# Attention recurrence of an adaLN block: layernorm moved into the loop, weights loaded ahead, deferred transposes cut into single pieces

## The chip, the cores and the metric

One core of one Trainium2 chip. The time is device time in microseconds (us) of one execution of the whole program, forward and backward. A program on one core has no other core to be compared with, so a run counts as slow only if it is over 1.5% above the fastest of the same kernel; every run used below counts as fast, save the single run of e5, whose state is unknown. The engines are TensorE (PE in the profile), VectorE (DVE), ScalarE (ACT), GpSimd (POOL) and SyncE (SP, which here only issues transfers).

## The reference, cut

```python
def _A_ref(x, mem0, Wq, Wk, Wv, Wo, seg_len):        # S=2048, Dm=512, H=32 heads, Dh=128, M=8, seg_len=32
    mem = mem0
    for s in range(n_seg):                           # 64 segments, one after another
        h = concatenate([mem, xs])                   # 8 memory rows + 32 rows of x
        q, k, v = h @ Wq, h @ Wk, h @ Wv
        p = softmax(where(mask, q k^T * scale, -1e9))
        o = (p v) @ Wo
        mem = o[:, :M, :].copy()                     # the next segment needs this
        outs.append(o[:, M:, :])
    return concatenate(outs)

mod = (silu(c) @ w_mod)...                           # sa, ca, ga, sb, cb, gb
h = layernorm(x) * (1 + ca) + sa
x = x + ga * _A_ref(h, ...)
h = layernorm(x) * (1 + cb) + sb
x = x + gb * _B_ref(h, w_gate, w_up, w_down)         # gated MLP
# the kernel returns x and the gradients of eleven inputs for a given grad_out
```

## The kernel before

Five phases matter by name. Phase 0 makes the modulation vectors from `w_mod`. Phase 1 makes the layernorm of all 2048 rows. Phase 2 is the recurrence of 64 segments. Phase 3 is the gated MLP, and what follows is the backward pass. Each phase opens pools of on-chip memory and closes them at its end, so a later phase's tiles lie over an earlier phase's, and a load into them waits until the earlier readers are done (before the change, the first projection waited 43.1 us for Wq, and POOL 8.2 us for a phase 1 transfer before it issued Wv).

```python
    def phase1(self):                                   # all 16 tiles ahead of the first segment
        ...
        for j in range(NT):
            nc.vector.tensor_scalar(xh[:], xall[:, j, :], mv[:, j, 0:1], rstd[:, j:j + 1], ...)
            nc.gpsimd.tensor_tensor(h1a[:], xh[:], ca1_bc[:], op=ALU.mult)
            nc.vector.tensor_tensor(h1[:], h1a[:], sa_bc[:], op=ALU.add)
            ...                                         # 4 transposes, one ACT copy
            nc.sync.dma_start(self.HX[s], hx[:, :, ...])   # to DRAM, one piece per segment

    def phase2(self):
        with ExitStack() as ctx:
            wp = ctx.enter_context(tc.tile_pool(name="p2w", bufs=1))   # over phase 0's and 1's memory
            nc.sync.dma_start(Wq[:], ...)               # 4 MB each
            nc.scalar.dma_start(Wk[:], ...)
            nc.gpsimd.dma_start(Wv[:], ...)
            nc.sync.dma_start(Wo[:], ...)
            ...
            for s in range(NS):
                ...
                nc.gpsimd.dma_start(self.MEMT[s], hT[:, :, 0:M])
                ...
                proj_bank("q", 0, QT, hT, "act")        # 48 matmuls of 40 columns, then an eviction
                proj_bank("k", 0, KT, hT, "dve")
                ...                                     # q1 k1 scores(0) q2 k2 scores(1)
                proj_bank("v", 0, VT, hT, "act"); den(0); st_exp(2)
                proj_bank("v", 1, VT, hT, "act"); den(1)
                proj_bank("v", 2, VT, hT, "act")
                vst(0); den(2); vst(1)                  # transposes of V, copied by DVE
                filler()                                # f_pst: all 3 thirds of P
                vst(2)
                pv(0); pv(1)                            # P times V, normalised by DVE into Ost
                filler()                                # f_qst: all 3 thirds of Q, copied by DVE
                pv(2)
                ott(0)                                  # transposes of Ost, copied by ACT into OT
                filler()                                # f_kst: all 3 thirds of K, copied by DVE
                ott(1); filler(); ott(2)
                outproj(0); outproj(1); outproj(2)
                nc.scalar.activation(hT_next[:, :, 0:M], at_ps[0][:, :, 0:M], AF.Copy)   # the recurrence
                ...                                     # AOT, VT and OT to DRAM
                fillers = mk_fillers()                  # [f_pst, f_qst, f_kst] of this segment
```

A filler is work of the last segment that nothing in the loop needs, kept for a place where TensorE would otherwise wait: transposes of P, Q and K for the backward pass, with a copy and a 384 KB store of each. VT and OT are stored in the same size, so a segment writes 5 x 384 KB, 1.97 MB. Of the names in the profiles, `proj_ps`, `tps`, `or_ps` and `at_ps` are what TensorE writes: projections, transposes, P times V and the output projection. An eviction is the copy of such a result by ACT or DVE. `Vst` is V transposed, `Ost` the normalised P times V, `OT` its transpose, which the output projection reads, and `hT` holds a segment's input rows.

The softmax here doesn't subtract the row's maximum and nothing guards it: scores larger than these inputs give would overflow.

## Time and profile before

| | before |
|---|---|
| time, median of the first 6 runs | 4554.05 us (4544.21 to 4566.25) |
| time, median of 16 runs beside the changed kernel | 4556.27 us |
| profiled execution | 4561.1 us |
| start, to the memory store of segment 1 | 175.8 us |
| 62 segment periods | 22.44 us each |
| border: last memory store to the first row tile of phase 3 | 49.0 us |
| everything after | 2944.8 us |

The last four rows come from the times at which single instructions start; the prediction shows the two memory stores, and the border ends where ACT writes `a_rows` at 1616.32. The granted TensorE clock was 0.50 from 50 to 150 us, and the first projection's matmuls, from 151.57 us on, issued every 33 ns. The loop alone, in the columns of the prediction's table of stretches:

```profile
175.00:1570.00 1395.00, 1216.81 (x38571) 1163.58 (x38568) 552.98 (x1304) 431.33 (x932) 245.58 (x436) 1.00 0.27 94
```

TensorE's waits between 500 and 1300 us, about 36 segments (what waited, for whom, us in total, times, longest):

```profile
PE tps L343 <- DVE Ost L391: 31.8, 72, 0.7
PE proj_ps L331 <- issue: 28.5, 35, 2.0
PE or_ps L389 <- DVE Vst L383: 25.6, 36, 0.7
PE proj_ps L331 <- ACT hT L445: 10.3, 36, 0.3
```

Lines 1, 3 and 4 are dependencies: each occurs once or twice in every segment and is short. Line 2 has no releaser that the profile shows.

### The profile page before, as it was taken

How to read it: one execution, taken by the hardware profiler on the slowest of the kernel's cores; microseconds unless marked ns; L12 is line 12 of the kernel's file. 1: busy time of each engine (PE TensorE's matmuls, PEld its weight loads, DVE VectorE, ACT ScalarE, POOL GpSimd, SP SyncE). 2: the span in 40 equal slices, each digit the busy share in tenths (PEclk: the TensorE clock that was granted, in tenths of full speed). 3: DMA queues.
4: the chain of work that ended last, by engine and by line, in shares of the span. 5: the costliest groups of instructions: out<-in, count | busy, mean ns of one | idle time of the engine just before them, and what ended most of it. 6: DMA issues, size and time to landing. Idle time of an engine off the chain costs nothing. (4 is left out here: it accounts for less than half of the span.)

```text
span 4561.1 us, 189989 instructions
## 1 busy us (share of the span) xinstructions
PE 3818.3 (84%) x87954; PEld 3203.8 (70%) x87954; DVE 1928.3 (42%) x4034; ACT 1498.9 (33%) x2570; POOL 820.2 (18%) x1210
## 2 busy tenths in 40 slices
PE   2588888888888868797878888888888858999996
PEld 1588888888888734453468888888888855666653
DVE  5234434433333455571123333333334326566554
ACT  0233333333333245351132222222222216565553
POOL 3011111111111111242101111111111122222210
PEclk6799999999999989898969999999999979999998
DMA  4522222222222399666754544544545468878773
GB/s 100 196 93 93 97 94 96 97 97 96 93 93 94 113 211 188 216 212 185 192 167 145 158 159 145 159 159 153 165 146 157 156 137 179 164 159 160 158 160 114
DMA packets 633321, 656.43 MB, mean 144 GB/s; under 512 B 429943, under 2 KB 516487, under 8 KB 630733
## 3 DMA queue, kind: packets, MB, share of 16 engines
q1 hardware_dynamic: 552396, 326.23, 29.9%
q0 software_dynamic: 75952, 304.94, 20.2%
q8 instruction: 687, 11.26, 1.1%
q10 hardware_dynamic: 4176, 13.11, 0.8%
q14 instruction: 110, 0.89, 0.1%
HBM read 346.57 MB, written 297.56 MB: 141 GB/s over the span
## 5 line engine op out<-in xcount | busy, mean ns | idle before, releaser
L1193 PE MATMUL gps<-rows,hrows 128*128 128x384 bf16 (+1 forms) x2640 | 461.7, 321 | 4.1 <-ACT ot L61 2.4
L1193 PEld LDWEIGHTS <-hrows 128*128 128x128 bf16 x2640 | 252.7, 98 | 139.3 <-issue 5.9
L1007 PE MATMUL dh_ps<-dKT,WkT 128*128 128x40 bf16 x8192 | 238.2, 183 | 109.9 <-issue 109.8
L1052 DVE CAST dh1T<-dh_ps 128x128 bf16<-128x128 f32 x64 | 18.7, 292 | 733.9 <-ACT dyT L1041 733.9
L331 PE MATMUL proj_ps<-hT,Wq 128*128 128x40 bf16 x8192 | 241.3, 180 | 84.0 <-DMA Wq<-in_A_Wq_dram 43.1
L1007 PEld LDWEIGHTS <-WkT 128*128 128x128 bf16 x8192 | 229.1, 98 | 115.1 <-issue 115.0
L63 DVE CAST KT<-proj_ps 128x480 bf16<-128x480 f32 (+2 forms) x256 | 119.7, 488 | 449.1 <-PE proj_ps L331 449.1
L63 DVE COPY rows<-tpg 128x384 bf16<-128x384 bf16 (+1 forms) x616 | 195.5, 347 | 262.9 <-PE tpg L1186 166.5
L331 PEld LDWEIGHTS <-Wq 128*128 128x128 bf16 x8192 | 228.4, 96 | 92.6 <-issue 92.6
L1007 PE MATMUL dh_ps<-dQT,WqT 128*128 128x40 bf16 x8192 | 240.6, 185 | 27.4 <-issue 26.5
L331 PE MATMUL proj_ps<-hT,Wk 128*128 128x40 bf16 x8192 | 241.1, 180 | 25.2 <-issue 24.6
L1007 PEld LDWEIGHTS <-WqT 128*128 128x128 bf16 x8192 | 232.0, 100 | 30.7 <-issue 30.5
L1007 PE MATMUL dh_ps<-dVT,WvT 128*128 128x40 bf16 x8192 | 238.5, 179 | 6.4 <-issue 6.0
L331 PEld LDWEIGHTS <-Wk 128*128 128x128 bf16 x8192 | 221.6, 96 | 29.0 <-issue 28.8
L331 PE MATMUL proj_ps<-hT,Wv 128*128 128x40 bf16 x8192 | 237.0, 179 | 4.3 <-issue 3.5
L1179 ACT ACTIVATE xr<-xt 128x3072 bf16<-128x3072 bf16 (+1 forms) x44 | 235.2, 5348 | 10.7 <-DMA x<-in_A_x_dram 5.7
L957 PEld LDWEIGHTS <-WoT 128*128 128x128 bf16 x8192 | 218.1, 96 | 26.0 <-issue 24.8
L957 PE MATMUL proj_ps<-dyT,WoT 128*128 128x40 bf16 x8192 | 219.8, 180 | 19.6 <-ACT dyT L1041 18.0
L1186 PEld LDWEIGHTS <-xr 128*128 128x128 bf16 x2560 | 179.9, 98 | 77.8 <-issue 28.2
L1007 PEld LDWEIGHTS <-WvT 128*128 128x128 bf16 x8192 | 226.9, 96 | 7.6 <-issue 7.1
L1186 PE MATMUL tpg<-ident,xr 128*128 128x128 bf16 x2560 | 217.6, 219 | 17.4 <-DVE rows L63 5.8
L331 PEld LDWEIGHTS <-Wv 128*128 128x128 bf16 x8192 | 225.6, 96 | 7.0 <-issue 5.9
(318 smaller groups left out, 7559.0 us busy)
## 6 DMA issues: line engine op xcount, KB each, us to landing
VT<-VT POOLq DMA_DIRECT2D x64, 384.0 KB, 3.2
OT<-OT POOLq DMA_DIRECT2D x64, 384.0 KB, 3.6
PS<-Pst POOLq DMA_DIRECT2D x64, 384.0 KB, 2.6
QST<-Qst POOLq DMA_DIRECT2D x64, 384.0 KB, 2.7
KST<-Kst POOLq DMA_DIRECT2D x64, 384.0 KB, 5.8
OT_l<-OT SPq DMA_DIRECT2D x64, 384.0 KB, 3.7
VT_l<-VT SPq DMA_DIRECT2D x64, 384.0 KB, 4.6
Pst_l<-PS SPq DMA_DIRECT2D x64, 384.0 KB, 5.1
```

Source lines behind the costliest of these rows:

```text
L63: return nc.vector.tensor_copy(out, in_)
L331: nc.tensor.matmul(ps[:, g_, hl * L:(hl + 1) * L], lhsT=Ws[w][:, c, h * E:(h + 1) * E], rhs=hT[:, c, :], start=(c == 0), stop=(c == DC - 1))
L957: nc.tensor.matmul(ps[:, g_, hl * L:(hl + 1) * L], lhsT=WoT[:, c, h * E:(h + 1) * E], rhs=dyT[:, c, :], start=(c == 0), stop=(c == DC - 1))
L1007: nc.tensor.matmul(dh_ps[0][:, c, :], lhsT=WT[:, h, c * 128:(c + 1) * 128], rhs=X[:, g_ * GW + hl * L:g_ * GW + (hl + 1) * L], start=(n_dh ...
L1052: nc.vector.tensor_copy(dh1T[:], dh_ps[0][:, :, M:L])
L1179: nc.scalar.activation(xr[:, 0:cut, :], xt[:, :, 0:cut].rearrange("p s x -> p x s"), AF.Copy)
L1186: nc.tensor.transpose(ps[0:KR, hl, :], xr[:, c0:c0 + 2, :].rearrange("p a s -> p (a s)"), self.ident[:, :])
L1193: nc.tensor.matmul(ps[:, 0:nh * E], lhsT=hrows[0:KR, tp_, c * 128:(c + 1) * 128], rhs=rows[0:KR, tp_, 0:nh * E], start=(tp_ == 0), stop=(t ...
```

## The change

Its intent is to start the recurrence before the whole layernorm is done, and to keep TensorE from waiting in the tail of a segment. Cut to its core:

```diff
+    def p2_early(self):                       # opened ahead of phase 0's pool: memory of its own
+        self.Wq = wp.tile(...); self.Wk = wp.tile(...)
+        self.ca1_bc = ...; self.sa_bc = ...; self.x_first = ...; self.mem0 = ...
+        self.p2tiles = [...]                  # QT KT VT ET Vst Ost OT Pst Qst Kst
+    def issue_early(self):                    # called right behind w_mod's load
+        nc.sync.dma_start(self.x_first[:], ...)
+        nc.sync.dma_start(self.mem0[:], ...)
+        nc.sync.dma_start(self.Wq[:], ...)
+        nc.sync.dma_start(self.Wk[:], ...)
 ...
-    def phase1(self):                         # all 16 tiles, HX through DRAM
+        def p1_tile(j):                       # one tile: 128 rows, 4 segments
+            nc.vector.bn_stats(...); nc.vector.bn_aggr(...); nc.vector.tensor_scalar_add(...)
+            nc.gpsimd.tensor_tensor(rstd[:], ve[:], mhalf[:], op=ALU.pow)
+            nc.vector.tensor_scalar(xh[:], ...)
+            nc.vector.tensor_tensor(h1a[:], xh[:], ca1_bc[:], op=ALU.mult)
+            nc.vector.tensor_tensor(h1[:], h1a[:], sa_bc[:], op=ALU.add)
+            ...                               # 4 transposes
+            for s4 in range(nseg):            # straight into the four segments' hT
+                nc.scalar.activation(t[:, :, cfg.M:cfg.L], tp[:, 0:DC, ...], AF.Copy)
 ...
-            nc.sync.dma_start(Wq[:], ...); nc.scalar.dma_start(Wk[:], ...)
             nc.gpsimd.dma_start(Wv[:], ...)
-            nc.sync.dma_start(Wo[:], ...)
+            nc.gpsimd.dma_start(Wo[:], ...)
 ...
             for s in range(NS):
+                if s % nseg_t == 2 and s // nseg_t + 1 < NT:
+                    p1_tile(s // nseg_t + 1)
                 ...
                 proj_bank("q", 1, QT, hT, "act")
+                filler()                      # P, first third
                 ...
                 proj_bank("q", 2, QT, hT, "act")
+                filler()                      # P, second third
                 ...
-                proj_bank("v", 0, VT, hT, "act")
+                proj_bank("v", 0, VT, hT, "dve")
+                filler()                      # P, last third, and its store
                 ...
-                proj_bank("v", 1, VT, hT, "act")
+                proj_bank("v", 1, VT, hT, "dve")
                 ...
                 vst(1)
+                vst(2)
                 filler()                      # Q, first third
-                vst(2)
                 pv(0)
+                filler()                      # Q, second third
                 pv(1)
+                pv(2)
                 filler()                      # Q, last third, and its store
-                pv(2)
                 ott(0)
                 filler()                      # K, first third
                 ott(1)
-                filler()
                 ott(2)
                 outproj(0); outproj(1); outproj(2)
                 ...                           # ACT copy of the memory rows
+                filler()                      # K, second third
+                filler()                      # K, last third, and its store
 ...
-                            self.evac("dve", part3(Qst, pi), ps[:, :, :])   # and Kst
+                            f_x(QT, Qst, self.QST, pi, "act")               # one third per filler, and Kst
```

## The prediction

> **What bounds the kernel now.** I read, in this order, the 40 slices (where is TensorE idle?), the table of stretches, the waits of the first 160 us, and one segment of the recurrence (phase 2) instruction by instruction. TensorE leads overall:
>
> ```profile
> PE 3818.3 (84%) x87954; PEld 3203.8 (70%) x87954; DVE 1928.3 (42%) x4034; ACT 1498.9 (33%) x2570; POOL 820.2 (18%) x1210
> PE   2588888888888868797878888888888858999996
> PEclk6799999999999989898969999999999979999998
> ```
>
> The change touches the first 14 slices only (phases 0, 1, 2) and the border to phase 3. By stretch (columns: length, busy time and count of each engine, granted clock, DMA share, GB/s):
>
> ```profile
> 0.00:160.00 160.00, 34.22 (x514) 22.54 (x515) 60.55 (x99) 13.46 (x21) 43.92 (x50) 0.62 0.57 173
> 160.00:1590.00 1430.00, 1248.07 (x39479) 1193.23 (x39477) 566.75 (x1337) 443.10 (x957) 249.39 (x443) 1.00 0.27 95
> 1590.00:1640.00 50.00, 16.63 (x90) 8.29 (x86) 18.06 (x35) 13.08 (x23) 8.06 (x15) 0.66 0.91 217
> ```
>
> So 160 us of start hold only 34 us of TensorE work. Then come 64 serial segments at 1248/1430 = 87% with DVE at 40% and ACT at 31%: TensorE is the bound there, and what can be won is its 13% of gaps. Why the start is empty:
>
> ```profile
> PE tp L229 <- DVE h L225: 67.9, 14, 32.7
> PE proj_ps L331 <- DMA Wq<-in_A_Wq_dram: 43.1, 1, 43.1
> POOL Wv L260 <- DMA hT<-HX: 8.2, 1, 8.2
> SPq L528 <- DMA KST<-Kst: 19.7, 2, 19.2
> ```
>
> Line 1 is phase 1, all 16 layernorm tiles before the first segment (61 to 116 us). Line 2: the four 4 MB weights are only issued at about 118 us, and the first projection starts at 151.57. Line 3 says why so late: the pool that holds the weights reuses memory of phases 0 and 1, and even Wv waits for a transfer that has nothing to do with it. Line 4 is the same effect at the border to phase 3. The tail of one segment:
>
> ```profile
> 835.41 0.38 PE L343 MATMUL tps<-ident,VT 128*128 128x128 bf16 x4
> 836.09 0.25 PE L376 MATMUL dc_ps<-ones,ET 128*128 128x1 bf16 x4 [0.30 <-ACT VT L61]
> 837.76 0.83 PE L343 MATMUL tps<-ident,QT 128*128 128x128 bf16 x12
> 839.23 0.38 PE L389 MATMUL or_ps<-Vst,ET 128*128 128x128 bf16 x4 [0.63 <-DVE Vst L383]
> 839.83 0.40 PE L343 MATMUL tps<-ident,Ost 128*128 128x128 bf16 x4 [0.22 <-DVE Ost L391]
> 842.02 0.40 PE L343 MATMUL tps<-ident,Ost 128*128 128x128 bf16 x4 [0.68 <-DVE Ost L391]
> 842.25 3.38 PE L408 MATMUL at_ps<-OT,Wo 128*128 128x40 bf16 x128
> 845.91 1.35 PE L331 MATMUL proj_ps<-hT,Wq 128*128 128x40 bf16 x48 [0.28 <-ACT hT L445]
> ```
>
> The segment runs from 824.26 to 845.91, 21.65 us. A 128-column transpose issues every 0.056 us and a 40-column matmul every 0.025 us; distances between the end of issue and the next start are the real holes: 0.46 before 836.09, 0.80 before 839.23, 0.38, 0.23 (at 840.96), 0.84 before 842.02 and 0.44 before 845.91, together 3.15 us. Pure issue is therefore 18.50 us. This segment has no "issue" holes; the mean period, from one store of the memory rows per segment,
>
> ```profile
> 175.84 0.72 POOL L358 DMA_DIRECT2D MEMT<-hT  x1 [2.25 <-ACT hT L445]
> 1567.30 0.72 POOL L358 DMA_DIRECT2D MEMT<-hT  x1 [1.68 <-ACT hT L445]
> ```
>
> is 1391.46 / 62 = 22.44 us, so irregular "issue" holes add about 0.8 us.
>
> [...] The trace shows 0.50 from 50 to 150 us and 33 ns per matmul at 151.57. [...] The 16.8 MB took about 44 us, some 380 GB/s, over three queues. [...]
>
> **The change part by part.**
>
> *Start.* Wq and Wk get memory of their own and are issued behind w_mod, at about 2 us. w_mod lands at 11.3; 8.4 MB at 380 to 420 GB/s then take 20 to 22 us: Wk is there at about 33. In parallel phase 0 ends with the last modbc copy at 29.3; ca and sa are copied by ACT instead of going through memory; layernorm of tile 0 can go ahead on DVE but for the affine part (two 0.69 us operations), then four transposes, four small copies: hT is ready near 31 to 32. First projection: about 33 us against 151.57. Wv and Wo wait for phase 0's pool, whose last reader is the modbc store; in the queue behind Wk it lands at about 38. Then 8.4 MB in about 21 us: Wv at about 49, Wo at 60. Segment 0 would reach v at 44 (11 us after its start, as before) and its output projection 9 us later, so it is held by both and ends near 63, against 175.3. **Saved: about 112 us.**
>
> *Phase 1 in the loop.* 15 tiles, each on DVE 0.66 + 0.17 + 0.15 + 0.55 + 0.69 + 0.69 = 2.9 us (rows L213, L214, and phase 3's twins L553, L558, L563, L565), 0.56 us of POOL (L555), four ACT copies of about 0.3 us (estimate from L445's 0.20 for a quarter of the columns) and 0.22 us of TensorE. On TensorE 0.06 us per segment. DVE and ACT have room, if the chain runs early. The order of an engine's queue isn't the source's: before, mem0's load (L308, phase 2) was issued at 1.65 us and the phase 2 memsets from 1.87. I expect the tile's DVE work to be moved up into idle time a segment or more ahead, and its transposes to find h1 ready. The HX store and loads vanish.
>
> *Segment.* Removed from DVE: six copies (2 x 1.07 us). Added to it: two V casts (2 x 0.66). Added to ACT: six copies of 0.60, removed two of 0.57. DVE is then near 8.7 us, ACT near 9.4 of some 20 us: neither binds on average. The real change is order. Pst (3 x 0.62) leaves the place ahead of Vst; Qst and Kst leave the place ahead of Ost. I walked the tail with the trace's delays (end of issue to result 0.16, hand-over 0.05 to 0.09). From the last V projection at 0: vst(2) waits for its ACT eviction to 0.75 (hole 0.21); Vst is done at 1.6, pv(2) needs it at 1.85, no hole; Ost results at 2.30, 2.90, 3.50 give holes 0.06, 0.16, 0.38 between the fillers; ACT does Q0, Q1, Q2, OT0, K0, OT1, OT2 one after another from 1.44, so OT0 is out at 3.84, a hole of 0.12 before the output projection at 3.89; OT1 (5.04) and OT2 (5.64) come before they are needed. Together 0.93 instead of 2.71. The two fillers after the output projection (0.44 us) fill the wait for hT almost exactly: 0.02. Period: 18.50 + 0.06 + 0.93 + 0.02 + "issue" 0.9 (a guess: as now, a little more under denser issue) = 20.4. **Saved: 2.04 x 64 = about 130 us.**
>
> *Border to phase 3.* TensorE rests from 1590.3 to 1615.6, since phase 3's tiles lie over Kst and wait for its store, which shares the DMA with 5.4 MB of weights. In the new layout w_gate's and w_up's place is over Wq and Wk, free since the last k projection some 15 us earlier, so the weights can be in flight sooner and the store lands sooner. I book 10 us of the 25.
>
> Sum: 112 + 130 + 10 = 252; 4554 - 252 = **4302 us**.
>
> **The rivals.** (a) *Layernorm on the path*: if the tile's chain stays at its place in the source, it starts behind the last segment's DVE work; about 4.3 us of chain then stand before q of every fourth segment: 15 x 4.5 = 67 us given back, 4370. For: single buffers, and POOL's queue, in which pow could sit behind a store that waits 11.6 us for V. Against: the reordering seen above. One in six. (b) *Fetch-bound*: [...] if "issue" holes grow to 2 us, half the segment gain goes: 4360. For: they sit 3 to 8 us into a segment, when the OT and KST stores run, which stay there. Against: 0.8 us now at nearly full issue. (c) *ACT the new bound in the tail*: seven evictions of 0.60 in a row have 0.6 us of slack at OT2; with one more late, 0.3 to 0.6 us per segment, 4320 to 4340. (d) *Better*: moved-up fillers close the remaining 0.9 us and the border gives 20 us: 4250.
>
> **Range and chances.** The start is worth 105 to 117 and nearly certain. The segment is worth 0.8 to 2.6 us times 64, 50 to 165. The border 0 to 20. That makes 4255 to 4375 for 8 in 10. The 2% line is 4463: even the start alone brings 2.5%, so faster has 0.96.
>
> **What would show it.** First projection between 31 and 36 us and segment 1 starting at 60 to 66: start right. Period from the MEMT stores 20.0 to 20.9, no Vst wait before the last pv, ET/QT/KT transposes in fours: segment right. A TensorE wait of microseconds for h1 in segments 2, 6, 10 would show rival (a); "issue" sums well above 0.8 us per segment rival (b); outproj waiting for ACT OT rival (c). The prediction fails if a wait on memory reuse holds Wq or the first tile as before, or if the period stays above 21.5.

## The result, and the profile after

The changed kernel took 4342.07 us in the median of 8 runs (4333.62 to 4351.64; a ninth, 4362.86, out of the median). The ratio is 0.9527, with a 95% interval from 0.9509 to 0.9546: faster. Here and below a ratio is the mean time of one kernel's fast runs over that of the other's fast runs of the same rounds on the same chip, so it is not quite the ratio of the medians quoted.

Between the two profiled executions, 4561.1 and 4339.9 us, the 221.2 us divide so:

| part | before | after | gained | predicted |
|---|---|---|---|---|
| start, to segment 1 | 175.8 | 69.1 | 106.8 | 112 |
| 62 periods | 22.44 each | 21.00 each | 89.6 | 126 (130 for 64) |
| border | 49.0 | 39.8 | 9.2 | 10 |
| unchanged code after it | 2944.8 | 2929.2 | 15.6 | 0 |

The last row is no gain. The same code took 2912 to 2952 us in the runs below, with no order in it. Between these two profiles the difference is about that of one group, the backward pass's own 40-column matmuls (`dh_ps<-dKT,WkT`): idle time in front of it that the profile calls "issue" was 109.9 us before and 93.7 after.

**The start.** TensorE from 24 to 72 us after the change (start, duration, what, in brackets the idle time before it and what ended it):

```profile
31.23 1.35 PE L347 MATMUL proj_ps<-hT,Wq 128*128 128x40 bf16 x48 [0.36 <-DVE hT L331]
...
32.85 1.37 PE L347 MATMUL proj_ps<-hT,Wk 128*128 128x40 bf16 x48 [0.27 <-DMA Wk<-in_A_Wk_dram]
...
52.34 1.78 PE L347 MATMUL proj_ps<-hT,Wv 128*128 128x40 bf16 x48 [11.84 <-DMA Wv<-in_A_Wv_dram]
...
64.08 4.45 PE L425 MATMUL at_ps<-OT,Wo 128*128 128x40 bf16 x128 [3.12 <-DMA Wo<-in_A_Wo_dram]
```

The first projection starts at 31 us instead of 152. Wk just about arrives in time; Wv costs 11.84 us and Wo 3.12, the two waits that the prediction had put there.

**The loop.** The same instruction as in the prediction's pair of memory stores, and the table's row of the loop:

```profile
69.05 0.73 POOL L375 DMA_DIRECT2D MEMT<-hT  x1 [6.02 <-ACT hT L465]
...
1370.95 0.72 POOL L375 DMA_DIRECT2D MEMT<-hT  x1 [1.74 <-ACT hT L465]
```

```profile
69.00:1370.00 1301.00, 1209.49 (x38482) 1164.85 (x38478) 560.82 (x1137) 551.66 (x1235) 251.74 (x447) 0.98 0.32 102
```

62 periods take 1301.90 us, 21.00 each. TensorE is busy for 93% of them instead of 87%, ACT for 42% instead of 31%, and the granted clock fell from 1.00 to 0.98. One tail, where the prediction shows that of before:

```profile
831.77 0.39 PE L406 MATMUL or_ps<-Vst,ET 128*128 128x128 bf16 x4
831.99 0.39 PE L359 MATMUL tps<-ident,QT 128*128 128x128 bf16 x4
832.22 0.61 PE L406 MATMUL or_ps<-Vst,ET 128*128 128x128 bf16 x8
832.66 0.39 PE L359 MATMUL tps<-ident,QT 128*128 128x128 bf16 x4
...
834.14 0.40 PE L359 MATMUL tps<-ident,Ost 128*128 128x128 bf16 x4 [0.20 <-DVE Ost L408]
834.37 3.38 PE L425 MATMUL at_ps<-OT,Wo 128*128 128x40 bf16 x128
837.60 0.61 PE L359 MATMUL tps<-ident,KT 128*128 128x128 bf16 x8
...
838.26 1.36 PE L347 MATMUL proj_ps<-hT,Wq 128*128 128x40 bf16 x48
```

No line waits for Vst or for the memory rows (hT) any more. One wait for Ost is left, and the output projection follows at once: OT is there. The last eight K transposes stand where TensorE used to wait for hT. By the same arithmetic as in the prediction (distance of starts less 0.0556 us for each 128-column matmul), the holes of this tail from pv on are 0.06, 0.14 and 0.38 us; the walk had 0.06, 0.16 and 0.38, and another 0.12 before the output projection, which is not there. TensorE's waits, same window as before:

```profile
PE proj_ps L347 <- issue: 38.3, 39, 2.7
PE tps L359 <- DVE Ost L408: 7.6, 38, 0.2
PE st_ps L387 <- issue: 3.7, 2, 2.0
```

The dependencies have shrunk to one regular line of 7.6 us. "issue" has grown from 28.5 to 38.3 us on the projections and is now nearly all that is left.

To have one measure for all runs I took, from every pair of neighbouring TensorE matmuls in the loop, the distance of starts less the pure issue time (the distance in an unbroken run at full clock, in these traces 0.025 us for 40 columns, 0.052 for 120, 0.0556 for 128) and summed what exceeds 0.06 us, by releaser. In us per segment:

| | period | waits for DVE | for ACT | "issue" | stretches at half clock in the loop |
|---|---|---|---|---|---|
| before | 22.44 | 2.14 | 0.69 | 1.10 | 2 |
| after | 21.00 | 0.66 | 0.12 | 1.40 | 12 |
| after, a second profile (e12) | 20.68 | 0.68 | 0.12 | 1.13 | 8 |

**The border.** SP issues `w_gate` at 1380.57 us, in the v stage of the last segment, where before it was issued at 1588.29, after the last segment; ACT writes the first `a_rows` at 1410.75 instead of 1616.32.

**What an "issue" hole is.** The longest kind, after the change:

```profile
905.44 0.18 PE L347 MATMUL proj_ps<-hT,Wk 128*128 128x40 bf16 x1
907.80 1.40 PE L347 MATMUL proj_ps<-hT,Wk 128*128 128x40 bf16 x47 [2.17 <-issue]
```

A projection stops after one of its 48 matmuls, in a tile that has all its inputs. Three things in the trace name the place. First, TensorE's 87,954 matmuls with a weight load each are 175,908 instructions, and the queue that the profile marks "instruction" moved 687 packets of 16 KB, one for 256 of them. In the loop it moved 301, for 38,482 matmuls, one for 128. So I call 128 matmuls a block, and its packet the fetch. Second, of the 62 holes over 0.6 us in the loop, 55 start at the same matmul number modulo 128, which I take for a block's border. Third, such a hole ends 1.4 us after such a packet has landed, in 9 of 10 cases between 1.20 and 1.59. The transfers around this hole, in 40 slices of 0.15 us from 902 us on, and the queues that moved them:

```profile
GB/s 0 41 41 27 27 0 41 178 0 0 451 205 532 369 287 205 0 41 0 41 314 123 0 0 0 0 0 0 41 0 0 0 41 0 41 0 41 0 0 0
...
q0 software_dynamic: 147, 0.45, 34.4%
q8 instruction: 1, 0.02, 1.3%
```

By this count TensorE entered the block before at 902.13. From 903.5 to 904.4, and once more at 905, q0 moves the stores of the segment's end. The one packet of q8 starts at 905.10, lands at 906.33, and the matmuls go on at 907.80. Over the loop, the packet starts 1.0 us (median) after the previous border where no hole follows and 1.6 us where one of over 0.3 us does, and it takes 1.15 us on average without such a hole, 1.40 before one. My estimate from these times is a chain: from border to border 1.0 + 1.15 + 1.4, about 3.6 us, while 128 matmuls of 40 columns issue in 128 x 0.025 = 3.2 us. A stretch of pure projections would then already be a little too fast for its own instructions, and a fetch that starts late would make a hole. What starts a packet, the trace does not show. After some of the long holes the clock then is at half for 3.4 us: 11 of the 12 such stretches in the loop begin within 5 us of an "issue" hole of 1.3 to 2.9 us. Another 14 holes of 1.3 to 2.3 us were followed by none; what decides is not shown.

### The profile page after: what moved, and what is told of

Its sections match the earlier page's. It is cut to its first block, busy times and chain, and to the rows that moved or that the text cites.

```text
span 4339.9 us, 189896 instructions
## 1 busy us (share of the span) xinstructions
PE 3805.6 (88%) x87954; PEld 3204.1 (74%) x87954; DVE 1904.9 (44%) x3809; ACT 1616.7 (37%) x2876; POOL 806.1 (19%) x1210
## 5 line engine op out<-in xcount | busy, mean ns | idle before, releaser
L1029 PE MATMUL dh_ps<-dKT,WkT 128*128 128x40 bf16 x8192 | 237.4, 183 | 93.7 <-issue 93.5
L388 ACT ACTIVATE ET<-st_ps 128x480 bf16<-128x480 f32 x192 | 109.5, 570 | 314.6 <-PE st_ps L387 314.6
```

The lines of the kernel that those rows point to most:

```text
L388: nc.scalar.activation(part3(ET, pi)[:, :, 0:120], st_ps[:, :, 0:120], AF.Exp, scale=cfg.scale)
L1029: nc.tensor.matmul(dh_ps[0][:, c, :], lhsT=WT[:, h, c * 128:(c + 1) * 128], rhs=X[:, g_ * GW + hl * L:g_ * GW + (hl + 1) * L], start=(n_dh ...
```

## The experiments

My theory was that the start and the segment give independent gains, that the order of the fillers gives most of the segment's, and that the missing 40 us are blocks of instructions fetched late while the segment's stores run. The rivals were: layernorm in the loop costs the 40 us; the exchange of engines, not the order, gives the gain; "issue" holes are a matter of density alone, whatever the stores do. All kernels gave the reference's result, save the one said to be wrong. Their columns:

| kernel | median us (runs' range) | ratio to before [95%] | period | DVE | ACT | "issue" | half clock |
|---|---|---|---|---|---|---|---|
| e1 | 4434.29 (4427.73 to 4442.22) | 0.9746 [0.9720, 0.9772] | 22.57 | 2.17 | 0.61 | 1.23 | 3 |
| e2 | 4432.74 (4411.10 to 4444.03) | 0.9740 [0.9707, 0.9773] | 20.54 | 0.52 | 0.13 | 1.11 | 9 |
| e3 | 4367.29 (4346.95 to 4375.06) | 0.9595 [0.9565, 0.9625] | 21.34 | 1.25 | 0.13 | 1.24 | 10 |
| e4 | 4399.40 (4385.31 to 4407.33) | 0.9669 [0.9644, 0.9694] | 21.90 | 1.49 | 0.85 | 0.96 | 6 |
| e5 | 4443.15 (1 run, loop only) | none | 20.45 | 0.64 | 0.12 | 0.97 | 7 |
| e6 | 4402.90 (4394.17 to 4412.50) | 0.9634 [0.9612, 0.9656] | 21.58 | 0.67 | 0.12 | 1.80 | 20 |
| e7 | 4354.45 (4347.66 to 4366.93) | 0.9523 [0.9502, 0.9544] | 21.03 | 0.62 | 0.13 | 1.48 | 11 |
| e9 | 4369.75 (4366.65 to 4376.61) | 0.9563 [0.9545, 0.9581] | 20.97 | 0.59 | 0.12 | 1.40 | 10 |
| e10 | 4298.02 (4289.29 to 4304.45) | 0.9486 [0.9465, 0.9508] | 20.31 | 0.59 | 0.12 | 0.91 | 5 |
| e11 | 4295.63 (4287.33 to 4306.83) | 0.9482 [0.9459, 0.9506] | 20.31 | 0.56 | 0.13 | 0.92 | 5 |
| e12 | 4310.84 (4308.41 to 4315.36) | 0.9515 [0.9496, 0.9535] | 20.68 | 0.68 | 0.12 | 1.13 | 8 |

e1 to e4 ran on one chip (the kernel before: 4547.56 us there), e5 to e9 on another (4574.7), e10 to e12 on a third (4533.48). Compare ratios across chips, not times. The "issue" column is from one profile each: kernels with the same order and the same stores in the loop (the change, e7, e9, e12) range from 1.13 to 1.48, so a smaller difference between two single profiles says nothing.

### e1: everything but the segment

The changed kernel with the loop body and fillers of before.

```diff
-                proj_bank("v", 0, VT, hT, "dve")     # and v1; fillers of one third each, on ACT
+                proj_bank("v", 0, VT, hT, "act")     # the whole body as before:
+                    return [f_pst, f_qst, f_kst]     # three whole fillers, on DVE
```

> The changed kernel with the segment of before (three large fillers at their old places, V evicted by ACT, Q and K copies on DVE); the early weights, the layernorm in the loop and the new memory layout stay. My accounting from the two traces: start 107 us, 62 segment periods 90 us, border 9 us, the rest chance. So I expect the period back at 22.3 to 22.6 us and a time of 4555 - 107 - 9 = 4425 to 4445. Rival: the layernorm tile in the loop costs something that the new fillers hide; then the period is over 22.8 us and the time over 4455.

A hit. Start, border and layernorm in the loop are worth 2.5%, some 115 us. The period is 22.57 us against 22.44 before. The difference of 0.13 us per segment is no more than that of "issue" (1.23 against 1.10), so layernorm in the loop costs little, and rival (a) of the prediction is out.

### e2: the new segment alone

The kernel before with the changed loop body and fillers; phase 1 and the loads stay as they were.

```diff
-                    return [f_pst, f_qst, f_kst]
+                    return [f_pst(0), f_pst(1), f_pst(2), f_x(QT, Qst, self.QST, 0, "act"), ...]   # and the changed body
```

> The kernel before with only the new segment (nine small fillers, engines exchanged); start, layernorm phase and memory layout as before. If the parts add: period 20.9 to 21.1 us, time 4556 - 92 = 4455 to 4475. Rival: the loop's layernorm and its DMA reads are what lengthened the issue holes (1.05 to 1.40 us per segment); then the period is 20.6 or less and the time under 4450.

A miss on the good side: 2.6%, some 118 us, and a period of 20.54. It is nearly what the prediction had for the segment (2.04 us saved; here 1.90), and it is the outcome that the rival had named. The two parts together make 5.1%, the whole change 4.7%. The difference of 0.4% is about as large as the intervals. The rival's cause, that layernorm in the loop feeds the "issue" holes, is not shown: they are 1.11 here, 1.40 and 1.13 with it, and they are not denser in the segments that hold a layernorm tile. This stays open.

### e3 and e4: order and engines apart

e3 has the new order with the old engines, e4 the old order with the new engines; both have the new start.

```diff
 e3:
-                proj_bank("v", 0, VT, hT, "dve")     # and v1
+                proj_bank("v", 0, VT, hT, "act")
-                            f_x(QT, Qst, self.QST, 0, "act"), ...     # all six
+                            f_x(QT, Qst, self.QST, 0, "dve"), ...
 e4:
-                proj_bank("v", 0, VT, hT, "act")     # and v1, in e1's kernel
+                proj_bank("v", 0, VT, hT, "dve")
-                            self.evac("dve", part3(Qst, pi), ps[:, :, :])     # and Kst
+                            self.evac("act", part3(Qst, pi), ps[:, :, :])
```

> The changed kernel with the nine small fillers at the new places, but Q and K copies on DVE and V evictions on ACT as before. Theory: most of the gain is that Pst, Qst and Kst left the places ahead of Vst and Ost on DVE in the tail; with Q and K copies (0.36 us each) back between the Ost operations on DVE the tail loses 3 to 4 of them, so period 21.5 to 22.0, time 4375 to 4410. Rival: only the order counts and DVE has room; then 21.0 us and 4342, same as the changed kernel.

> The changed kernel with the three large fillers at their old places, but Q and K copies on ACT and V evictions on DVE as in the change. Theory: DVE ahead of Vst still has three Pst (1.87 us), but Ost no longer waits behind Qst and Kst; on ACT, OT now waits behind three Q and three K copies (1.8 us each), which holds the output projection. I expect little or nothing of the gain: period 21.9 to 22.6, time 4400 to 4445. Rival: the engines alone give most of it; then period under 21.5 and time under 4375.

The order alone brings 0.9746 to 0.9595, the exchange alone to 0.9669. Both are real, and they overlap: the exchange on top of the order adds only 0.7% (0.9595 to 0.9527). e3 came out a little better than I expected, and so did e4: 21.90 and 4399 lie at the edge of the forecast, but "little or nothing of the gain" was wrong, since against e1 it gains 0.8%. Why the exchange still counts shows on DVE in e3:

```profile
815.28 0.42 DVE L63 COPY Qst<-tps 128x512 bf16<-128x512 bf16 x1
815.62 0.68 DVE L408 TENSOR_TENSOR Ost<-or_ps,rden 120x512 bf16<-120x512 f32 x1
816.22 0.41 DVE L63 COPY Qst<-tps 128x512 bf16<-128x512 bf16 x1
```

The Q copies stand between the normalisations of Ost, and TensorE's next transposes wait for Ost, so the DVE holes are 1.25 us instead of 0.66. In e4 the waits are the old ones and a new one:

```profile
PE or_ps L406 <- DVE Vst L400: 26.5, 37, 0.7
...
PE at_ps L425 <- ACT OT L61: 10.9, 37, 0.3
```

Vst costs what it cost before (25.6), because P still stands ahead of it; and OT, which waited for nobody before, now queues behind the Q and K copies on ACT. That is rival (c) of the prediction. It exists, but only without the new order.

### e5 and e6: the stores of Q and K taken out of the loop, and doubled

e5 keeps the transposes and copies and moves the two stores behind the loop (with stale data: its result is wrong, and some 130 us of stores follow the loop, so only the loop is read). e6 stores Q and K twice.

```diff
 e5:
-                            if pi == NP - 1:
-                                nc.gpsimd.dma_start(dram[s], gl3(dst))
+            for s in range(NS):                      # after the loop
+                nc.gpsimd.dma_start(self.QST[s], gl3(Qsts[s % 2]))
+                nc.gpsimd.dma_start(self.KST[s], gl3(Ksts[s % 2]))
 e6:
                                 nc.gpsimd.dma_start(dram[s], gl3(dst))
+                                nc.gpsimd.dma_start(dram[s], gl3(dst))
```

> The changed kernel without the QST and KST stores inside the loop (the last tiles are stored 64 times after it, so that later phases read numbers; the result is wrong on purpose, and some 130 us of stores are added after the loop, so only the loop is read). TensorE's issue holes fall on its instruction blocks' borders: 301 blocks of 128 matmuls in 62 segments, the holes all at the same place modulo 128, 1.4 us after a 16 KB fetch has landed. Theory: [...] with 768 KB less per segment the issue holes fall from 1.40 to 0.9 us per segment or less, the half-clock episodes from 13 to 4 or fewer, and the period from 21.0 to 20.2 to 20.5 us. Rival: the fetch itself (about 1.1 us to start, 1.15 us to move, 1.4 us until used) is too slow for 128 matmuls in 3.2 us, whatever else moves; then holes stay at 1.2 to 1.5 and the period at 20.8 to 21.1.

> The changed kernel with each QST and KST store issued twice (same bytes to the same place; the result stays right). Theory of contention: issue holes of 1.8 us per segment or more, period 21.5 to 22.2, time 4375 to 4420. Rival (fetch too slow by itself): period 20.9 to 21.1, time 4335 to 4355.

TensorE's first wait in e5, then in e6, in the window 500 to 1300 us (28.5 before, 38.3 after the change):

```profile
PE proj_ps L347 <- issue: 28.2, 36, 2.2
```

```profile
PE proj_ps L347 <- issue: 49.2, 46, 2.3
```

With 768 KB less stored per segment the "issue" holes are 0.97 us, with the usual stores 1.13 to 1.40 (the two profiles of the changed kernel), with 768 KB more 1.80; the half-clock stretches go from 7 over 8 to 12 to 20. The dependencies do not move (0.62 to 0.68 on DVE). TensorE's instructions are the same in all of them. On the chip of e5 and e6 the usual stores gave 1.48 (e7) and 1.40 (e9). So the stores lengthen the holes at the borders: density alone does not set them. e5 is a hit on the period but not on the holes (0.9 or less and 4 stretches expected): 0.97 us stays without these stores. The estimate of 3.6 against 3.2 us would leave some holes; three other stores stay in the loop too.

### e7: the same stores in thirds

If a backlog of one large store were to blame, three small ones, each issued as soon as its third is ready, would help.

```diff
-                            if pi == NP - 1:
-                                nc.gpsimd.dma_start(dram[s], gl3(dst))
+                            nc.gpsimd.dma_start(dram[s][:, pi * PG:(pi + 1) * PG, :], part3(dst, pi))
```

> The changed kernel with the PS, QST and KST stores each split in three, one as soon as a third of the tile is there, so that the same bytes leave more evenly. If the backlog of whole 384 KB stores is what delays a fetch: issue holes 0.9 to 1.2, period 20.5 to 20.8, time 4315 to 4330. If only the total of bytes counts: same, 4335 to 4350. If [...] POOL with six more issues a segment becomes late: slower, over 4355.

0.9523 and a period of 21.03: the same as the change itself. The size of one store is not the matter.

### e9: Wv among the early weights

Wv holds the first segment for 11.84 us. Here it gets memory of its own and is issued right behind Wk.

```diff
+        self.Wv = wp.tile([128, DC, H * E], BF16, name="Wv")          # in p2_early
+        nc.sync.dma_start(self.Wv[:], ...)                            # in issue_early, behind Wk
-            nc.gpsimd.dma_start(Wv[:], ...)
```

> The changed kernel with Wv too in memory of its own, issued behind Wk at the start. In the changed kernel the first segment waits 11.8 us for Wv and 3.1 us for Wo. Wk landed at 32.9, so Wv lands at about 43 and v starts at 43 instead of 52.3; Wo, issued at 38 as now, lands at about 54 while the output projection wants it at about 53. Segment 1 then starts 9 to 10 us sooner (59 to 60 instead of 69), time 4330 to 4335. Rival: the MODBC store waits behind Wv in its queue and Wo with it, so that the first output projection waits longer; then the gain is 0 to 5 us.

A miss, and in the other direction: segment 1 starts at 82.6 us instead of 69.1. DVE and TensorE say why:

```profile
DVE maskT L298 <- DMA MODBC<-modbc: 17.5, 1, 17.5
```

```profile
PE p1tp L269 <- DVE ve L257: 23.7, 1, 23.7
```

The store of the modulation rows stands on the same issuing queue behind the weights and lands at 46.7 us instead of 37.3. DVE's write of `maskT`, which lies over phase 0's memory, waits for that store, and the first layernorm tile now starts behind it on DVE (46.94 us; in the changed kernel it had started at 18.14). Whether the tile's own working memory also lies over phase 0's now, or only its place in DVE's queue holds it, the trace does not tell. I had moved one wait by 4 MB and laid another across the first tile. The border was 47.2 us as well, against 39.8.

### e10, e11 and e12: the stores of O and K moved away from the start of the segment

The holes sit mostly 2 to 8 us into a segment (after the change, 61 of the 74 over 0.3 us at a block's border), where q and k are projected and the stores of OT (end of the segment before) and K (behind its last filler) are under way. e10 issues both behind the store of P instead, about 12 us into the segment, where transposes and score matmuls lie between the projections and a block lasts longer (after the change, the matmuls of a block that starts 11 to 15 us into a segment take 4.79 us to issue in the median; those of a block that ends 2 to 8 us into it, 3.20 to 3.66). TensorE's order is the same, matmul for matmul. e11 adds Wv and Wo on SP's queue. e12 is the changed kernel again, for the comparison on one chip.

```diff
-                nc.gpsimd.dma_start(self.OT[s], gl3(OT))
 ...
-                            if pi == NP - 1:
+                            if pi == NP - 1 and dram is self.QST:
                                 nc.gpsimd.dma_start(dram[s], gl3(dst))
 ...                                                     # in the filler of P's last third:
-                                nc.gpsimd.dma_start(self.PS[s], gl3(Pst))
+                                ins = nc.gpsimd.dma_start(self.PS[s], gl3(Pst))
+                                with tc.issue_after(getattr(ins, "ins", ins)):
+                                    nc.gpsimd.dma_start(self.OT[s], gl3(OTs[i2]))
+                                    if s > 0:
+                                        nc.gpsimd.dma_start(self.KST[s - 1], gl3(Ksts[1 - i2]))
 e11 besides:
-            nc.gpsimd.dma_start(Wv[:], ...); nc.gpsimd.dma_start(Wo[:], ...)
+            nc.sync.dma_start(Wv[:], ...); nc.sync.dma_start(Wo[:], ...)
```

> The changed kernel with the same stores of the same bytes, but OT and KST are queued behind the next segment's PS store, so that they leave beside the v projections and the tail and not beside the output projection and the q and k projections, where an instruction block lasts only 3.2 to 3.5 us. TensorE's order is the same, instruction for instruction. Theory (a fetch is late when a store backlog meets the short blocks): issue holes 0.9 to 1.15 us per segment instead of 1.40, period 20.5 to 20.75, ratio to the changed kernel of the same chip 0.993 to 0.996. Rival (only the bytes count, as the split stores suggested): same holes at other places, ratio 0.999 to 1.002.

> The late stores, and Wv and Wo issued from SP's queue instead of POOL's, at the same time (38 us), so that Wv comes whole before Wo. From POOL the two took 38 to 63.5 us, 340 GB/s; Wq and Wk came at 420 GB/s from SP. Expected: Wv at 48 instead of 52, Wo at 58 instead of 63.5, segment 1 at 63 to 65 instead of 69, another 4 to 6 us below the late stores. Rival: SP's queue holds Wv behind the first layernorm rows' store and load, or layernorm tile 1 behind Wo, so nothing or a loss.

> The changed kernel itself again, as the measure for the two others on this chip and for how much its issue holes vary from run to run: ratio to before 0.951 to 0.955, issue holes 1.2 to 1.6 us per segment.

The loop of e10, TensorE's first wait in the same window as above, and the two memory stores:

```profile
69.00:1328.00 1259.00, 1199.76 (x38494) 1156.75 (x38492) 559.84 (x1132) 551.62 (x1236) 250.64 (x446) 0.99 0.29 105
```

```profile
PE proj_ps L347 <- issue: 22.8, 33, 1.9
```

```profile
68.95 0.73 POOL L375 DMA_DIRECT2D MEMT<-hT  x1 [1.95 <-ACT hT L465]
...
1328.37 0.72 POOL L375 DMA_DIRECT2D MEMT<-hT  x1 [3.70 <-ACT hT L465]
```

The period is (1328.37 - 68.95) / 62 = 20.31 us, the "issue" holes 0.91 us, with the same bytes stored. Against the changed kernel of the same chip (e12) the mean of the runs is 4298.12 over 4311.36, 0.9969, and the slowest run of e10 (4304.45) is faster than the fastest of e12 (4308.41): about 13 us, a little less than I expected. The loop itself is 23 us shorter than e12's (1259.4 against 1282.1); in the profiles the unchanged code after it took 12 us longer, which is in the scatter told above. e12 missed its own forecast of the holes (1.13 against 1.2 to 1.6), and 0.91 against 1.13 is no larger a difference than between profiles of one kernel; but e11, with the same late stores, has 0.92, and all nine runs of e10 and e11 are faster than all four of e12. e10 is faster than both kernels of this study. e11 is a miss: Wv reached TensorE at 51.9 us and Wo at 64.7, as on the other queue, and its time is that of e10. In the changed kernel Wv came at about 420 GB/s and Wo at 350, and in e11 the same, so here the start was held by the transfers themselves, not by who issued them. Why Wo came more slowly is not shown.

## Why the prediction was right, and where its sum was off

The range held (4342 in 4255 to 4375); the point, 4302, was 40 us low. By the prediction's own steps:

1. *Start, 112 us.* Right: 106.8. First projection 31.2 (33 predicted), Wv at 52.3 (49), Wo at 64.1 (60). The 5 us are the two loads: their bytes flowed from about 40 us instead of 38, and Wo at only 350 GB/s where 380 to 420 were booked.
2. *Layernorm in the loop, 0.06 us per segment of TensorE.* Right in kind. TensorE never waited for h1 in the loop, and each later tile's transposes were issued about two segments before they were needed. e1's period is 0.13 us longer than before's, within what the "issue" holes vary. Rival (a), one in six, did not occur.
3. *Tail, 0.93 + 0.02 us of dependency holes.* Right in kind and nearly in size. Three of the walk's holes came out within 0.02 us; that of vst(2) was 0.12 instead of 0.21, and the 0.12 before the output projection did not occur. Over all segments 0.66 + 0.12 = 0.78 us are left of 2.83. e3 and e4 show that the order did most of it and that each half of the change alone leaves one of the old waits.
4. *"issue" 0.9 us, "a guess: as now, a little more under denser issue".* This is the term that was mis-sized. "As now" was already read too small: 0.8 us came from one segment whose dependency holes, 3.15 us, were above the mean of 2.83, while over all segments the "issue" holes before were 1.10. After the change they measured 1.40 us (1.13 in the second profile), and with them came something that I had not booked: 12 stretches at half clock instead of 2, each 3.4 us long. By the distances of starts TensorE issues 1.1 us less in such a stretch than at full clock, 12 x 1.1 / 62 = 0.21 us per segment. Together the period is 18.50 + 0.06 + 0.78 + 1.40 + 0.21 = 20.95, against 21.00 measured and 20.4 predicted. 0.6 us over 62 periods are 37 us, nearly the whole of the miss. (The start and the border lost 6 us more and the factor of 64 instead of 62 another 4; the unchanged code gave some of it back by chance.) The prediction had larger "issue" holes as rival (b) and priced them at 4360; the 40 us that came of it are two thirds of the 58 between that and 4302. That the denser issue made the holes grow is not shown: e2, with the new segment, has 1.11, as before the change, and e1, with the old waits, 1.23.
5. *Border, 10 us.* Right: 9.2. The new memory layout brings it: the border is 38.8 us in e1, with the new layout and the old segment, and 47.7 in e2, the other way round.

Shown by intervention: the stores' share of the "issue" holes (e5, e6, e10, all with TensorE's work unchanged). Inferred from times in the trace: that these holes are late blocks, and the estimate of 3.6 us. Not shown: how much of the difference between 1.10 and 1.40 is the change's, as the same order and stores gave 1.13 to 1.48. Not seen: why a fetch starts late, since the trace has no record of what a packet waits for. Open: the 0.4% by which the parts' sum exceeds the whole.

## What to carry to other kernels

Where an engine waits in every turn of a loop, walk one turn instruction by instruction: whole fillers that stand ahead of a short dependent copy make the wait they were meant to fill, and the same filler in thirds, on the engine that the path did not need just then, filled most of it here (2.83 us of waits for DVE and ACT per segment before, 0.78 after). Where TensorE runs long stretches of small matmuls, as here 128 of 40 columns in 3.2 us, look for "issue" holes and for the stores that run beside them; moving two stores by half a segment was worth 0.3% here, without touching TensorE. And before a load is moved ahead, ask which later tile now lies over the memory that it gave up, as e9 did not.
